# First group's x in four transfers, its statistics and normalization spread over other engines

## The chip, the core and the metric

The kernel runs on one NeuronCore of a Trainium2 chip. The metric is device time in microseconds (us) of one execution, the median of several runs. TensorE (PE in the profile, PEld for its weight loads), VectorE (DVE), ScalarE (ACT), GpSimd (POOL) and SyncE (SP, which here issues all transfers) each work through their own instructions in order, and wait for each other through semaphores.

## What is computed

x is 2048 tokens of 448 features. `xn` is its layer normalization over the features. The output is x + A(xn) + B(xn):

```python
# A: global filter in the frequency domain
X = rfft2(xn); y = irfft2(X * (w_r + 1j * w_i), s=(S, D))
# B: spatial-shift token mixing, then a channel MLP
h  = gelu(layernorm(xn) @ w1)                    # 448 -> 448
hs = concat(shift(h quarter 0, +1), shift(quarter 1, -1),
            shift(quarter 2, +2), shift(quarter 3, -2)) @ w2
x1 = xn + hs
out_B = x1 + gelu(layernorm(x1) @ w3) @ w4       # 448 -> 1792 -> 448
```

## The kernel before

Tokens are dealt to 16 blocks of 128 tokens, `xb(b)`, so that a shift by one token is a shift by one block. Two neighbouring blocks share a tile `xt`. Stage B goes by groups of four blocks: `GRP = [[14, 15, 0, 1], [2, 3, 4, 5], [6, 7, 8, 9], [10, 11, 12, 13]]`. Each fp32 operand of a matrix product is split into an fp16 high half and an fp16 low half, and a product is three matmuls (high by high, high by low, low by high).

Ahead of a split, a weight matrix is scaled by a power of two. `squares` sums its squares on ScalarE, one ACTIVATE and one accumulator read for each part. `powers` adds the sums (`tensor_reduce`, L243 on VectorE), spreads the total over the partitions with a matmul by ones (L245, here "the ones-matmul"), and makes the powers `s` and `r` in three small VectorE steps (L249 to L252). This happens four times, for w1, w2, w3 and w4 (s1 to s4).

The stretch that matters is the front:

- `load_x(0)` loads the four blocks of group 0 in two transfers (L192), then come w1 in four parts, the next groups' x, w2 and w3, all on SP's one queue.
- TensorE meanwhile runs `WARM` matmuls on zeros (L752).
- `norm1(g, apply)` normalizes a group: `stats` takes mean and variance of each block on VectorE (`bn_stats` L289, `bn_aggr` L290), five small steps (L306 to L311) make an approximate scale and a bias, and `apply` names the engine that applies them to each block (L319 on VectorE or POOL, L316 on ScalarE). The function `refine`, some ten small POOL steps (L328 to L337), makes the exact scale later.
- `T1(g)` transposes a group in four quarters of the features on TensorE (`pta`, L370). ScalarE copies each quarter as the high half of `xT` (L374), VectorE subtracts it for the low half (L375).
- `split_w` makes the halves of w1. For the first two quarters ScalarE scales and rounds (L264) and VectorE makes the low half (L265). For the last two POOL scales in place (L260), ScalarE rounds (L261) and POOL subtracts (L262). w2's four quarters all go by POOL.
- `w1_in` runs group 0's 44 matmuls (L410) into four banks. `w1_unit` applies gelu and splits h, and a transposing DMA (L434) turns h around. Then group 1 follows in the same way, and group 2.
- `w2_tile(b)` multiplies the four shifted quarters of h with w2 (L450), in the order 2, 0, 1, 3.

Much later come the MLP (L381, L716), then A, and the last MLP groups. L697 there splits the MLP's hidden tile.

The order on each engine is fixed when the program is built: a scheduler places the instructions by priority and by an estimate of its own, and `with behind(key):` keeps the instructions of a block behind a named earlier one on the same engine, for example

```python
    with behind("n", 0):
        s1, r1 = powers(m1, 4, "1", "mm")
```

keeps s1's steps behind group 0's applies on VectorE. So an edit at the front can move instructions further on in the order.

Of the kernel before, what the change touches and what calls it, by code (L numbers as in the profile page):

```python
# [23 lines left out]
CS = {b: 4 * g + i for b, (g, i) in WHERE.items()}  # L24
PASS = ((0, 0), (0, 1), (1, 0))
SHIFT = [1, -1, 2, -2]
WARM = 28
ZPRE = 2.0 ** -7
UPRE = 2.0 ** -3
VPRE = 2.0 ** -3  # L30
# [89 lines left out]
def body(tc, nc, x, wf, w1, w2, w3, w4, c_g, c_n, c_small, out):  # L120
    V, A, P, T, SY = nc.vector, nc.scalar, nc.gpsimd, nc.tensor, nc.sync
# [50 lines left out]
    xr = pw.tile([128, 904], F32, name="xr")  # L172
# [13 lines left out]
    ident = pc.tile([128, 128], F32, name="ident")  # L186
# [1 line left out]


    def load_x(g):  # L190
        for b0 in sorted(GRP[g])[::2]:
            SY.dma_start(xt[b0 // 2], xv[:, b0:b0 + 2])  # L192

    load_x(0)
    w1s = stage("w1s", F, 0).rearrange("p (t n) -> p t n", t=4)
# [38 lines left out]
    def squares(col, src, junk=None):  # L234

        n = src.shape[-1]
        junk = xr.bitcast(F16) if junk is None else junk
        A.activation(out=junk[:src.shape[0], :n], in_=src, func=AF.Square, scale=2.0 ** -20, accum_out=col)

    def powers(m, n, key, tag="acc"):  # L240

        t = pc.tile([128, 2], F32, name=f"pt{key}")
        V.tensor_reduce(out=t[:, 0:1], in_=m[:, :n], axis=AX.X, op=ALU.add)  # L243
        pm = bank(tag, f"pm{key}") if isinstance(tag, str) else tag
        i = T.matmul(pm[:, 0:1], ones, t[:, 0:1], start=True, stop=True)  # L245
# [5 lines left out]
        V.tensor_scalar(out=e[:, 1:2], in0=e[:, 0:1], scalar1=-1, scalar2=185 << 23, op0=ALU.mult, op1=ALU.add)  # L251
        V.tensor_scalar(out=e[:, 2:3], in0=e[:, 0:1], scalar1=1, scalar2=69 << 23, op0=ALU.mult, op1=ALU.add)  # L252
        return e.bitcast(F32)[:, 1:2], e.bitcast(F32)[:, 2:3]

    def absmax(out_, in_):
# [1 line left out]

    def split_w(hi, lo, src, s, low=None):
        if low is P:
            P.tensor_scalar(out=src, in0=src, scalar1=s, scalar2=0.0, op0=ALU.mult, op1=ALU.add)  # L260
            i = A.activation(out=hi, in_=src, func=AF.Copy)  # L261
            j = P.tensor_tensor(out=lo, in0=src, in1=hi, op=ALU.subtract)  # L262
            return i.ins, j.ins
        i = A.activation(out=hi, in_=src, func=AF.Copy, scale=s)  # L264
        j = V.scalar_tensor_tensor(out=lo, in0=src, scalar=s, in1=hi, op0=ALU.mult, op1=ALU.subtract)  # L265
        return i.ins, j.ins
# [17 lines left out]
    def stats(src, key, mv=None):  # L284
        if mv is None:
            mv = pc.tile([128, 4, 2], F32, tag="mv", bufs=3, name=f"mv{key}")
        for i, s in enumerate(src):
            st = pc.tile([128, 6], F32, tag="st", bufs=4, name=f"st{key}_{i}")
            V.bn_stats(out=st, in_=s)  # L289
            V.bn_aggr(out=mv[:, i, :], in_=st)  # L290
        return mv
# [5 lines left out]
    def norm1(g, apply):  # L297

        bs = GRP[g]
        n, b0 = len(bs), bs[0]  # L300
        mv = pc.tile([128, 4, 2], F32, name=f"mva{b0}")
        stats([xb(b) for b in bs], f"a{b0}", mv)
        a = pc.tile([128, 2 * n], F32, name=f"va{b0}")
        yi = pc.tile([128, 2 * n], I32, name=f"vy{b0}")
        y = yi.bitcast(F32)
# [5 lines left out]
        i = V.scalar_tensor_tensor(out=nm, in0=mv[:, :n, 0], scalar=-1.0, in1=y[:, n:], op0=ALU.mult, op1=ALU.mult)  # L311
        after["c", g] = (i.ins,)
        for k, b in enumerate(bs):
            y_, m_ = y[:, n + k:n + k + 1], nm[:, k:k + 1]
            if apply[k] is A:
                i = A.activation(out=xb(b), in_=xb(b), func=AF.Identity, scale=y_, bias=m_)  # L316
                after["na", g] = (i.ins,)
            else:
                i = apply[k].tensor_scalar(out=xb(b), in0=xb(b), scalar1=y_, scalar2=m_, op0=ALU.mult, op1=ALU.add)  # L319
# [4 lines left out]
        w, r = (pc.tile([128, 2 * n], F32, name=f"v{t}{b0}") for t in "wr")  # L324
# [38 lines left out]
    def transpose_split(srcs, dst, key, ts=range(4), at=0, tags=("tr",) * 4):  # L363
        c = slice(128 * at, 128 * at + 128 * len(srcs))
        for t in ts:
            pt = bank(tags[t], f"pt{key}{t}")
            w = 128 if t < 3 else 64
            with behind("T", key) if ("T", key) in after else contextlib.nullcontext():
                for i, s in enumerate(srcs):
                    m = T.transpose(pt[:w, 128 * i:128 * i + 128], s[:, 128 * t:128 * t + w], ident)  # L370
            after["T", key] = (m.ins,)
            pt = pt[:w, :128 * len(srcs)]
            lo = dst[:, 4 + t, c] if t < 3 else dst[64:128, 3, c]
            i = A.activation(out=dst[:w, t, c], in_=pt, func=AF.Copy)  # L374
            j = V.tensor_tensor(out=lo, in0=pt, in1=dst[:w, t, c], op=ALU.subtract)  # L375
            after[key, t] = after[key] = i.ins, j.ins

    def mlp_in(ps_out, wp, cols, xT, tok, ts=range(4)):
        for t in ts:
# [305 lines left out]
    acc, hs, rest = {}, {}, {}  # L685
# [64 lines left out]
    def warm_up(n):  # L750
        for i in range(n):
            T.matmul(wps, wsrc[:, 0:128], wsrc, start=True, stop=True)  # L752
# [6 lines left out]
    xTs = {}  # L759
    flat = lambda t: t.rearrange("p a n -> p (a n)")  # L760

    def T1(g, ts=range(4)):
        if g not in xTs:
            xTs[g] = p1.tile([128, 7, 512], F16, tag="xT", bufs=2, name=f"xT{g}")
        transpose_split([xb(b) for b in GRP[g]], xTs[g], f"a{g}", ts,
                        tags=("mm", "mm", "tr", "tr") if g == 2 else ("tr", "tr", "acc", "acc"))

    def w3_split(i):
        t, cl = i % 4, slice(896 * (i // 4), 896 * (i // 4) + 896)
        split_w(w3p[:, t, cl], w3p[:, 4 + t, cl], w3raw[:, t, cl], s3)  # L770

    def w4_split(f):
        split_w(w4p[0][:, 0, f:f + 2], w4p[0][:, 1, f:f + 2], w4raw[:, f:f + 2], s4)

    for t in range(3):
        squares(m1[:, t:t + 1], w1s[:, t])
    squares(m1[:64, 3:4], w1s[:64, 3])
    n1 = [norm1(0, [P, V, A, V])]
    with behind("n", 0):
        s1, r1 = powers(m1, 4, "1", "mm")  # L780
    h_alloc(0)
    first = [bank("mm" if k < 2 else "sp", f"pw1_0{k}") for k in range(4)]
    for t in range(4):
        with behind("p1"):
            T1(0, [t])
        with behind("a0", t):
            after["w1", t] = split_w(w1p[:, t], w1p[:, 4 + t], w1s[:, t], s1, P if t > 1 else V)
    h1 = pc.tile([128, 1], F32, name="h1")
    V.tensor_scalar(out=h1, in0=s1, scalar1=2.0 ** -5, scalar2=None, op0=ALU.mult)
    for t in range(4):  # L790
        w1_in(0, list(enumerate(first)), [t])
    n1[0][0]()
    with behind("w1", 1):
        n1.append(norm1(1, [P, V, A, V]))
    with behind("w1", 3):
# [2 lines left out]
    with behind("n", 1):  # L798
        s2, r2 = powers(m2, 1, "2", first[0][:, 448:512])
# [28 lines left out]
    with behind("a2"):  # L828
        n1 = [norm1(3, [P, P, P, P])]
# [97 lines left out]
    bs = [*range(12, 16), *range(8, 12), *range(8)]  # L927
    for n in range(17):
# [4 lines left out]
        if n:  # L933
            b = bs[n - 1]
# [30 lines left out]
```

## Time and profile before

| | |
|---|---|
| median of 3 runs | 420.48 us (420.2 to 420.87) |
| the profiled execution | 420.4 us |
| its span in the profile | 418.6 us |
| TensorE matmuls | 409.8 us, 98% of the span |
| VectorE | 291.6 us, 70% |
| ScalarE | 248.1 us, 59% |
| GpSimd | 118.6 us, 28% |
| granted TensorE clock | 1.0 |

Busy time is the union of an engine's instructions over the whole span. A matmul's record is longer than its place in the stream, since matmuls overlap, so the share of TensorE is not a share of its peak. Times in the views count from the start of the span. A row of the timeline gives start, duration, engine, line, operation, the tiles out<-in with their shapes, and how many instructions it merges. A row of the chain of waits gives start, duration, and what the end of the program waited for in that time. In a row by window stand the window, its length, the busy time of PE, PEld, DVE, ACT and POOL, the granted clock, the DMA engines' share and their GB/s. A row of transfers ends with their size and the median us from issue to landing.

### The profile page before, as it was taken

Reading aid. Unit: us, or ns where it says so; the run is one execution under the profiler, and the core shown is the slowest. Engines: PE = TensorE matmul, PEld = TensorE weight load, DVE = VectorE, ACT = ScalarE, POOL = GpSimd, SP = SyncE. Lnnn points to the kernel's source line nnn. Section 1 sums busy time; section 2 is a strip of 40 time slices with the busy share of each in tenths; the row PEclk is TensorE's granted clock in tenths of the full one; section 3 lists DMA queues with packets and bytes.
Section 4 is the critical chain, followed back from the end, with each engine's and each line's share of the span. In section 5 each row is a group of like instructions: output and inputs, shape, how many; then the busy total and the mean of one; then the engine's idle time right before and its main releaser. Section 6 shows DMA issues by size and latency. Waiting matters only on the chain.

```text
span 418.6 us, 8535 instructions
## 1 busy us (share of the span) xinstructions
PE 409.8 (98%) x3329; PEld 291.7 (70%) x3329; DVE 291.6 (70%) x615; ACT 248.1 (59%) x428; POOL 118.6 (28%) x204
## 2 busy tenths in 40 slices
PE   7999999999999999999999999999999999999996
PEld 3655555765668777776887887777776767577785
DVE  4888899798774766652689889865999529942112
ACT  4698869972758866632678888864534414422331
POOL 3876700101345746300031221211454203200000
DMA  8959982734761365315056555610001003331001
GB/s 271 362 174 175 275 174 95 132 78 90 191 156 50 89 234 165 93 41 140 14 142 173 149 144 142 177 39 2 2 2 68 22 2 132 134 133 40 5 0 45
DMA packets 51832, 47.61 MB, mean 114 GB/s; under 512 B 33936, under 2 KB 47056, under 8 KB 51792
## 3 DMA queue, kind: packets, MB, share of 16 engines
q1 hardware_dynamic: 51792, 47.07, 41.7%
q8 instruction: 26, 0.43, 0.4%
q14 instruction: 14, 0.11, 0.1%
HBM read 35.52 MB, written 3.67 MB: 94 GB/s over the span
## 4 chain that ended last, share of the span: by engine, by line
PE 72%; DVE 14%; DMA 6%; issue 5%; POOL 1%; ACT 1%; SPq 1%; POOLq 0%; DVEq 0%
PE pw L381 25%; PE acc L716 22%; PE pw L450 7%; PE pw L410 6%; PE ps L536 3%; PE pu L638 2%; PE pp L593 2%; PE px L610 2%; DMA xr<-x 1%; DVE w4p L265 1%; DMA out<-xr 1%; PE pta L370 1%; DMA x2mem<-y 1%; DVE xt L682 1%; DVE sta L289 1%
## 5 line engine op out<-in xcount | busy, mean ns | idle before, releaser
L381 PE MATMUL pw<-x2mem,w3p 128*128 128x256 f16 x1232 | 151.8, 273 | 0.0
L716 PE MATMUL acc<-w4p,hf 128*128 128x448 f16 (+1 forms) x714 | 140.0, 341 | 0.7 <-DVE hf L697 0.7
L381 PEld LDWEIGHTS <-w3p 128*128 128x128 f16 x1232 | 118.9, 98 | 23.1 <-issue 0.9
L716 PEld LDWEIGHTS <-hf 128*128 128x128 f16 x714 | 69.2, 98 | 49.2 <-DVE hf L697 1.6
L697 DVE SCALAR_TENSOR_TENSOR hf<-pw,h,hf 128x512 f16<-128x512 f32 x56 | 41.7, 747 | 55.5 <-ACT hf L696 55.3
L694 ACT ACTIVATE pw<-pw,pe 128x512 f32<-128x512 f32 x56 | 36.6, 655 | 70.5 <-PE pw L381 69.4
L450 PE MATMUL pw<-w2p,h 112*128 112x448 f16 x192 | 40.1, 352 | 0.8 <-DMA h<-hs 0.8
L696 ACT ACTIVATE hf<-pw,h 128x512 f16<-128x512 f32 x56 | 38.3, 686 | 1.4
L619 POOL TENSOR_TENSOR z<-te 128x450 f32<-128x450 f32 x16 | 16.3, 1016 | 74.0 <-DVE te L617 74.0
L410 PE MATMUL pw<-w1p,xT 128*128 128x448 f16 x176 | 35.3, 352 | 0.0
L450 PEld LDWEIGHTS <-h 112*128 112x128 f16 x192 | 18.7, 98 | 17.0 <-DMA h<-hs 1.0
L666 POOL TENSOR_TENSOR e<-e 128x226 f32<-128x226 f32 x16 | 13.9, 866 | 56.5 <-ACT e L663 45.3
L410 PEld LDWEIGHTS <-xT 128*128 128x128 f16 x176 | 16.9, 98 | 16.2 <-DVE xT L375 0.8
L600 ACT ACTIVATE pf<-pp 64x450 f16<-64x450 f32 x32 | 17.3, 540 | 16.7 <-DVE pf L601 8.2
L601 DVE TENSOR_TENSOR pf<-pp,pf 64x450 f16<-64x450 f32 x32 | 19.9, 622 | 5.3 <-ACT pf L600 5.0
L663 ACT ACTIVATE e<-pe 128x452 f32<-128x452 f32 x16 | 8.7, 547 | 15.6 <-DVE vh L674 12.3
L516 POOL TENSOR_TENSOR xr<-xf 128x452 f32<-128x452 f32 x8 | 9.7, 1208 | 28.3 <-issue 22.9
L615 ACT ACTIVATE te<-px 64x450 f32<-64x450 f32 x32 | 17.2, 538 | 0.5
L673 ACT ACTIVATE vh<-e 128x448 f16<-128x448 f32 x16 | 9.2, 574 | 14.0 <-DVE e L671 8.3
L519 POOL TENSOR_TENSOR f<-xr 128x452 f32<-128x452 f32 x16 | 16.1, 1028 | 0.6
L527 DVE TENSOR_TENSOR xh<-f,xh 128x452 f16<-128x452 f32 x16 | 11.8, 780 | 5.9 <-ACT xh L526 5.9
L681 PE MATMUL py<-vh,csm 128*128 128x448 f16 x48 | 13.5, 352 | 1.5 <-DVE vh L674 0.7
(163 smaller groups left out, 602.8 us busy)
## 6 DMA issues: line engine op xcount, KB each, us to landing
wc<-wf SPq DMA_DIRECT2D x32, 225.0 KB, 3.7
wl<-wf SPq DMA_DIRECT2D x8, 450.0 KB, 3.7
xt<-x SPq DMA_DIRECT2D x8, 448.0 KB, 8.2
xf<-x SPq DMA_DIRECT2D x8, 448.0 KB, 3.7
w3raw<-w SPq DMA_DIRECT2D x3, 896.0 KB, 12.8
xr<-x SPq DMA_DIRECT2D x12, 224.0 KB, 2.6
out<-xr SPq DMA_DIRECT2D x12, 224.0 KB, 2.0
gn<-c_g SPq DMA_DIRECT2D x16, 128.0 KB, 3.3
```

The costliest lines, as they stand in the source:

```text
L381: T.matmul(ps_out, wp[:, wi + t, cols], xT[:, xi + t, tok], start=t == 0 and wi + xi == 0, stop=t == 3 and wi == 4)
L410: T.matmul(pm[:, :D], xTs[g][:, xi + t, 128 * i:128 * i + 128], w1p[:, wi + t], start=t == 0 and p == 0, stop=t == 3 and p == 2)
L450: T.matmul(pm[:, :D], hT[g][:112, 4 * hi + k, o:o + 128], w2p[:, wi, k], start=n == 0, stop=n == 11)
L519: P.tensor_tensor(out=f[:, :, k:k + 2].rearrange("p b s d -> p s b d"), in0=u[:, :, 0], in1=u[:, :, 1], op=op)
L600: A.activation(out=hi, in_=src, func=AF.Copy)
L601: V.tensor_tensor(out=lo, in0=src, in1=hi, op=ALU.subtract)
L615: A.activation(out=e[64 * h:64 * h + 64], in_=px_[64 - 64 * h:128 - 64 * h, :2 * DF], func=AF.Copy)
L619: P.tensor_tensor(out=z, in0=t[:, 0], in1=t[:, 1], op=ALU.add)
L694: A.activation(out=pm, in_=pm, func=AF.Gelu_apprx_tanh, scale=r3)
L696: i = A.activation(out=h[:, 0], in_=pm, func=AF.Copy, scale=h3)
L697: j = V.scalar_tensor_tensor(out=h[:, 1], in0=pm, scalar=h3, in1=h[:, 0], op0=ALU.mult, op1=ALU.subtract)
L716: m = T.matmul(to, h[:, hi, o:o + 128], w4p[0][:, wi, f, r], start=f == 0 and n == 0, stop=f == 13 and n == 2)
```

## The change

Six edits, all at the front:

1. Group 0's x comes in four transfers, one for each block, in the order 14, 15, 0, 1.
2. Block 14's mean and variance are taken by two ScalarE ACTIVATEs with accumulators (Identity, then Square with the mean as its bias). POOL turns the mean's sign and scale. VectorE's `bn_stats` takes the other three blocks.
3. The apply of block 0 moves from ScalarE to VectorE, so that POOL applies block 14 and VectorE 15, 0 and 1.
4. `T1` is cut into its TensorE part (`turn_pe`) and its copies (`turn_copy`). For group 0 the first quarter's transposes stand ahead of the ones-matmul of s1, and the other three quarters behind it. The copies of a quarter stand behind the weight split of the quarter before it, and the first behind s1.
5. POOL's scalings of w1 stand ahead of group 0's `refine` (`after["ws"]`).
6. w2's quarters are split in the order 2, 0, 1, 3, and `WARM` is 26 instead of 28.

```diff
-WARM = 28
+WARM = 26
...
     def load_x(g):
-        for b0 in sorted(GRP[g])[::2]:
-            SY.dma_start(xt[b0 // 2], xv[:, b0:b0 + 2])
+        for b0 in GRP[g][::1 if g == 0 else 2]:
+            if g == 0:
+                SY.dma_start(xb(b0), xv[:, b0])
+            else:
+                SY.dma_start(xt[b0 // 2], xv[:, b0:b0 + 2])
...
-        stats([xb(b) for b in bs], f"a{b0}", mv)
+        if g == 0:
+            t = pc.tile([128, 1], F32, name="ms")
+            junk = xr[:, 0:D]
+            A.activation(out=junk, in_=xb(b0), func=AF.Identity, scale=-D ** -1.5, accum_out=t)
+            A.activation(out=junk, in_=xb(b0), func=AF.Square, scale=D ** -0.5, bias=t, accum_out=mv[:, 0, 1:2])
+            P.tensor_scalar(out=mv[:, 0, 0:1], in0=t, scalar1=-D ** 0.5, scalar2=None, op0=ALU.mult)
+        stats([xb(b) if g or b != b0 else None for b in bs], f"a{b0}", mv)
...
+    def turn_pe(g, t):
+        pt = bank((("mm", "mm", "tr", "tr") if g == 2 else ("tr", "tr", "acc", "acc"))[t], f"pta{g}{t}")
+        w = 128 if t < 3 else 64
+        with behind("T", g) if ("T", g) in after else contextlib.nullcontext():
+            for i, b in enumerate(GRP[g]):
+                m = T.transpose(pt[:w, 128 * i:128 * i + 128], xb(b)[:, 128 * t:128 * t + w], ident)
+        after["T", g] = (m.ins,)
+        return pt[:w]
+
+    def turn_copy(g, t, pt):
+        ...
+        i = A.activation(out=dst[:w, t], in_=pt, func=AF.Copy)
+        j = V.tensor_tensor(out=lo, in0=pt, in1=dst[:w, t], op=ALU.subtract)
+        after[f"a{g}", t] = after[f"a{g}"] = i.ins, j.ins
...
+    n1 = [norm1(0, [P, V, V, V])]
     for t in range(3):
         squares(m1[:, t:t + 1], w1s[:, t])
     squares(m1[:64, 3:4], w1s[:64, 3])
-    n1 = [norm1(0, [P, V, A, V])]
-    with behind("n", 0):
+    pts = [turn_pe(0, 0)]
+    with behind("n", 0), behind("T", 0):
         s1, r1 = powers(m1, 4, "1", "mm")
+    with behind("p1"):
+        pts += [turn_pe(0, t) for t in range(1, 4)]
     h_alloc(0)
     first = [bank("mm" if k < 2 else "sp", f"pw1_0{k}") for k in range(4)]
     for t in range(4):
-        with behind("p1"):
-            T1(0, [t])
+        with behind(*(("w1", t - 1) if t else ("s1",))):
+            turn_copy(0, t, pts[t])
         with behind("a0", t):
             after["w1", t] = split_w(w1p[:, t], w1p[:, 4 + t], w1s[:, t], s1, P if t > 1 else V)
...
-    n1[0][0]()
+    with behind("ws"):
+        n1[0][0]()
...
     with behind("na", 2):
-        for k in range(4):
+        for k in (2, 0, 1, 3):
             split_w(w2p[:, 0, k], w2p[:, 1, k], w2s[:112, k], s2[:112], P)
```

More of the change, by code (lines that the diff above doesn't have):

```diff
@@ L251, in powers @@
         V.tensor_scalar(out=e[:, 1:2], in0=e[:, 0:1], scalar1=-1, scalar2=185 << 23, op0=ALU.mult, op1=ALU.add)
-        V.tensor_scalar(out=e[:, 2:3], in0=e[:, 0:1], scalar1=1, scalar2=69 << 23, op0=ALU.mult, op1=ALU.add)
+        i = V.tensor_scalar(out=e[:, 2:3], in0=e[:, 0:1], scalar1=1, scalar2=69 << 23, op0=ALU.mult, op1=ALU.add)
+        after["s" + key] = (i.ins,)
         return e.bitcast(F32)[:, 1:2], e.bitcast(F32)[:, 2:3]
@@ L259, in split_w @@
         if low is P:
-            P.tensor_scalar(out=src, in0=src, scalar1=s, scalar2=0.0, op0=ALU.mult, op1=ALU.add)
+            i = P.tensor_scalar(out=src, in0=src, scalar1=s, scalar2=0.0, op0=ALU.mult, op1=ALU.add)
+            after["ws"] = (i.ins,)
             i = A.activation(out=hi, in_=src, func=AF.Copy)
@@ L287, in stats @@
         for i, s in enumerate(src):
+            if s is None:
+                continue
             st = pc.tile([128, 6], F32, tag="st", bufs=4, name=f"st{key}_{i}")
@@ L361, in behind, with T1 @@
             yield
-    def transpose_split(srcs, dst, key, ts=range(4), at=0, tags=("tr",) * 4):
-        c = slice(128 * at, 128 * at + 128 * len(srcs))
-        for t in ts:
[L366 to L376, printed above, removed]
+    def turn_pe(g, t):
[7 more added lines that the diff above has]
+    def turn_copy(g, t, pt):
+        w = 128 if t < 3 else 64
+        if g not in xTs:
+            xTs[g] = p1.tile([128, 7, 512], F16, tag="xT", bufs=2, name=f"xT{g}")
+        dst = xTs[g]
+        lo = dst[:, 4 + t] if t < 3 else dst[64:128, 3]
+        i = A.activation(out=dst[:w, t], in_=pt, func=AF.Copy)
+        j = V.tensor_tensor(out=lo, in0=pt, in1=dst[:w, t], op=ALU.subtract)
+        after[f"a{g}", t] = after[f"a{g}"] = i.ins, j.ins
+    def T1(g, ts=range(4)):
+        for t in ts:
+            turn_copy(g, t, turn_pe(g, t))
     def mlp_in(ps_out, wp, cols, xT, tok, ts=range(4)):
@@ L760, in body @@
     flat = lambda t: t.rearrange("p a n -> p (a n)")
[L762 to L766, printed above, removed]
     def w3_split(i):
```

## The prediction

> **What bounds the kernel now.** I read the page's chain first, then what TensorE waited for, then the chain in order of time for the first 70 us, then each engine's timeline there. From the page, and TensorE's waits over the whole span:
>
> ```profile
> span 418.6 us, 8535 instructions
> PE 72%; DVE 14%; DMA 6%; issue 5%; POOL 1%; ACT 1%; SPq 1%; POOLq 0%; DVEq 0%
> PE pm L245 <- DVE pt L243: 1.0, 1, 1.0
> PE pw L450 <- DMA h<-hs: 0.8, 1, 0.8
> ```
>
> TensorE is the chain. Everything the change edits lies ahead of the end of the last wait shown. After that TensorE starts matmuls back to back until far behind the reordered stretch, so what the front gains or loses reaches the end unshortened, unless a new gap opens. The chain of waits in order of time:
>
> ```profile
> 1.19 4.32 DMA xt<-x
> 5.53 2.21 DVE sta L289 x4
> 7.74 0.29 DVE mva L290 x4
> 8.94 0.93 DVE xt L319 x2
> 9.99 0.38 PE pm L245 x2
> 10.37 1.94 PE pta L370 x16
> 12.31 8.41 PE pw L410 x44
> 30.45 3.20 DMA h<-hs
> ```
>
> x lands at 5.51; four statistics, the applies, the ones-matmul for w1's power of two (s1), 16 transposes; from 12.31 to 20.7 the 44 matmuls of group 0 run at 0.19 us each. So the front is worth what those 44, and what follows them, start earlier.
>
> **x and the applies.** The rows of the pieces that move, from the timeline:
>
> ```profile
> 0.73 0.87 SPq L192 DMA_DIRECT2D xt<-x  x2
> 1.22 7.74 PE L752 MATMUL wps<-wsrc 128*128 128x512 f16 x28 [1.22 <-DVE wsrc L183]
> 9.05 0.19 ACT L238 ACTIVATION_READ_ACCUMULATOR xr<-w1s 64x1 f32 x1
> 9.12 1.17 POOL L319 TENSOR_SCALAR xt<-xt,vy,nma 128x448 f32<-128x448 f32 x1
> 43.50 2.82 POOL L319 TENSOR_SCALAR xt<-xt,vy,nma 128x448 f32<-128x448 f32 x4
> ```
>
> SP issues four transfers where it issued two: two more at 0.44 us push the w1 issues back 0.9 us. Call x the delay with which the data then land. Block 14, the first, goes to ScalarE: two ACTIVATEs (0.6, like L374's below) with an accumulator read of 0.19 each, about 1.5 us, hidden by the wait for w1, whose squares are ScalarE's next work and whose data come after x; POOL's one small instruction for the mean (0.2) is hidden by the statistics. That cover holds while block 14 lands before 4.8; each us later than that would hold up the applies by one. VectorE does the other three as they land, so behind the last landing stands one statistic (0.55 a piece) where there were four: three less is 1.6, and three of the four aggregates 0.2. The applies start at 8.94-1.8=7.15+x. VectorE has three, one each 0.43 after the other, done at 8.5. POOL's apply of block 14 starts 0.19 later and takes 0.70 alone (2.82/4) and 1.17 beside two VectorE applies: 0.23 for each, 1.4 beside three, so it ends at 8.75+x. That cover is thin but costs nothing: the transposes that wait for it then run 8.8 to 9.3, while s1 is still to come. The 26 warm-up matmuls end two of 28 earlier (0.28 each on the mean), at 8.4: still ahead of those transposes, so they cost and bring nothing.
>
> **s1 and the weights.** The rows that carry the sum:
>
> ```profile
> 9.79 0.15 DVE L243 TENSOR_REDUCE pt<-m 128x1 f32<-128x4 f32 x1
> 10.79 0.15 DVE L251 TENSOR_SCALAR pe<-pe 128x1 int32<-128x1 int32 x1
> 11.04 0.60 ACT L374 ACTIVATE xT<-pta 128x512 f16<-128x512 f32 x1 [1.15 <-PE pta L370]
> 11.54 0.66 ACT L264 ACTIVATE w1p<-w1s,pe 128x448 f16<-128x448 f32 x1
> 12.28 0.68 DVE L265 SCALAR_TENSOR_TENSOR w1p<-w1s,pe,w1p 128x448 f16<-128x448 f32 x1
> 14.06 2.20 DVE L289 BATCH_NORM_STATS2 sta<-xt 128x6 f32<-128x448 f32 x4
> 14.51 1.25 POOL L260 TENSOR_SCALAR w1s<-w1s,pe 128x448 f32<-128x448 f32 x2
> 19.11 1.17 POOL L319 TENSOR_SCALAR xt<-xt,vy,nma 128x448 f32<-128x448 f32 x1
> 20.57 1.47 PE L370 MATMUL pta<-ident,xt 128*128 128x128 f32 x12
> 26.84 0.56 DVE L803 TENSOR_TENSOR s<-h,pe 128x1 f32<-128x1 f32 x1
> 27.33 0.15 DVE L804 SCALAR_TENSOR_TENSOR s<-pe,pe 128x1 f32<-128x1 f32 x1
> ```
>
> The last square of w1 is read at 9.24+x. L243 stood behind the applies until 9.79; now it starts at 9.27+x, and its chain of 1.15 us gives s1 at 10.42+x instead of 10.94. ScalarE has copied xT's first quarter before that (9.6 to 10.2), so its first w1 half starts with s1 and ends at 11.1+x instead of 12.2. TensorE does four transposes, the ones-matmul at 9.47+x (0.38), then twelve transposes at 0.12 (16 took 1.94): it reaches group 0's matmuls at 11.3+x instead of 12.3. So TensorE gains 1.0-x here.
>
> VectorE gains less. After s1 it does xT's low quarter (0.69, to 11.15+x), then w1's low half. But POOL's two scalings of w1 (L260, 0.63 each) move from 14.51 to right behind s1: 10.47 to 11.73+x. L803, 128x1, takes 0.56 us while POOL's scaling of w2 runs, its like L804 0.15: a VectorE instruction with two inputs in SBUF sits out the POOL instruction under way. w1's low half has two such inputs, so I let it wait until 11.73+x. At a pitch of 0.6 it, xT's second and w1's second low half follow, and group 1's statistics start at 13.5+x instead of 14.06: 0.57-x earlier. (The Trainium skill says this in "SBUF — State Buffer", section "Who interferes with whom": VectorE with two SBUF inputs and a GpSimd instruction that reads SBUF exclude each other, and whichever starts first holds the port to its end. It speaks against this change, and L803 agrees with it. Without the rule the sum would be 1.0-x.) From there VectorE's steps are the old ones, so POOL's apply of block 2, which ended at 20.28, ends at 19.7+x; group 1's transposes need it and start at 19.76+x. TensorE had finished group 0 at 19.57+x. Gain: 20.57-19.76-x = 0.8-x.
>
> **x.** Bounds: SP's lag of 0.9 if the issue decides, and about 0 if the transfers are simply full. What the queue moved, by window (the last column is GB/s):
>
> ```profile
> 3.00:3.50 0.50, 0.50 (x3) 0.21 (x2) 0.00 (x0) 0.00 (x0) 0.00 (x0) 1.00 1.14 394
> 5.00:5.50 0.50, 0.50 (x4) 0.20 (x3) 0.00 (x0) 0.00 (x0) 0.00 (x0) 1.00 1.03 301
> xr<-x SPq DMA_DIRECT2D x12, 224.0 KB, 2.6
> ```
>
> The first is x in rows of 3584 bytes, the second w1 in rows of 1792, as x's will be. All of x (0.92 MB) at 301 instead of 394 GB/s would be 0.7 us more. Against it, a lone 224 KB block of x elsewhere lands 2.6 us after its issue, so the first would be there at 3.3, and three more at 301 GB/s (0.76 each) make 5.6 for the last, 0.1 later than now. I take x=0.2, near this row, and the range 0 to 0.7.
>
> **w2's quarters, and where the stretch ends.**
>
> ```profile
> 31.20 1.04 POOL L262 TENSOR_TENSOR w2p<-w2s,w2p 112x448 f16<-112x448 f32 x1
> 32.42 3.01 POOL L262 TENSOR_TENSOR w2p<-w2s,w2p 112x448 f16<-112x448 f32 x3
> 33.16 2.67 SPq L434 DMA_TRANSPOSE h<-x2mem  x2
> 33.69 0.36 PE L450 MATMUL pw<-w2p,h 112*128 112x448 f16 x1 [0.77 <-DMA h<-hs]
> ```
>
> Each tile of w2 begins with quarter 2, whose low half was POOL's third; now it is ready at 32.2 instead of 34.4, and two more matmuls (0.38) fit into TensorE's wait. That buys nothing: the next blocks of h come from SP's transposes, one every 1.37 us, and before too TensorE met the fourth of them as it landed (issued 33.16). What counts is when the second was issued (30.45), and that hangs on VectorE, whose work the chain follows from group 1's transposes on nearly without a pause. The 0.8-x arrives there whole. Sum: 0.8-0.2=0.6. The profiled execution took 420.4 (span 418.6 and 1.8 around it); the median shown is 420.48. Forecast: 420.4-0.6=**419.8**.
>
> **Rivals.** (1) *The front gains fully*: VectorE's low half slips in ahead of POOL's scaling and x is 0. TensorE then sets the start: gain 1.0. In the mid part the only gap of note may also close:
>
> ```profile
> 121.58 1.69 PE L716 MATMUL acc<-w4p,hf 128*128 128x448 f16 x8 [0.38 <-DVE hf L697]
> ```
>
> 0.5 us with its start. 418.9 to 419.4. For it: only 0.1 us lies between the two starts in my sum. Against: POOL needs nothing but s1.
>
> (2) *It does nothing*: the data lag by the whole 0.9 us of issue. Gain 0.8-0.9: 420.5. For it: the transfers' ramp is slow, and if it counts rows and not bytes, half-size rows carry half as much. Against: the w1 data waited behind x, not for their issue. ("DMA: Bandwidth & Descriptors", section "Bandwidth", in the Trainium skill, asks for transfers of 1 MiB and more; by it four blocks lose against two. Here four in flight share one queue, and 2.6 us for a lone block is mostly latency.)
>
> (3) *Slower: a wait moves into the full stretch.* The built order changes from 31 to 125 us. The ones-matmul of w4's power of two (86.75 before) now stands behind 43 fewer matmuls of w3 (256 columns) and 11 fewer of w2 (448): at the 0.191 us that group 0's 448 columns take, and 0.109 for 256, 6.8 us earlier, at 80.0. It needs ScalarE's seventh square of w4 and VectorE's L243:
>
> ```profile
> 80.15 1.22 ACT L481 ACTIVATE y<-y,vs 128x448 f16<-128x448 f32 x2
> 82.11 0.19 ACT L238 ACTIVATION_READ_ACCUMULATOR xr<-x2mem 128x1 f32 x1
> 84.41 0.16 DVE L243 TENSOR_REDUCE pt<-m 128x1 f32<-128x7 f32 x1
> 86.75 0.28 PE L245 MATMUL pm<-pt,ones 128*128 128x1 f32 x2
> ```
>
> With these times TensorE would stand for 84.6-80.0=4.6 us: 424.4. But ScalarE's new order puts four normalizations (L481, 0.61 each) behind that square, which then is read at 82.3-2.4=79.9, and VectorE's order brings L243 forward behind it: just in time. Each us later than 80.0 costs one us; from 0.6 on the front's gain is gone. VectorE's 2.1 us between the read and L243 show how late it may come: a loss of up to 2.1-0.6=1.5, so 420.5 to 421.9.
>
> **The numbers.** Chances: forecast 0.45, (1) 0.30, (2) 0.08, (3) 0.17. 0.2% of 420.48 is 0.84 us, about what a measurement of this kernel can tell from no change. The forecast's own range (x 0 to 0.7) is 419.6 to 420.3, a gain of 0.1 to 0.8, inside the 0.84 but at its better end close to it; of its 0.45 I give 0.07 to the far side. Of (3)'s 0.17, 0.05 is a small loss within the 0.84. Faster 0.30+0.07=0.37, same 0.38+0.08+0.05=0.51, slower 0.12. The range 418.8 to 421.2 takes in (1), (2) and half of (3).
>
> **What would show it.** Right: group 0's first w1 matmul near 11.4, its transposes from 9.0, s1 near 10.6, group 1's transposes near 20.0, w1's first low half on VectorE over 1 us long, and behind 37 us no new gap on TensorE. Wrong: w1's squares read at or after 9.9 (my x too small); that low half no longer than L265's 0.68 and group 1's transposes at 19.6 (rival 1); a wait of TensorE on L246, the new line of L243, near 80 us (rival 3); a first w1 matmul slower than 0.19 us, which would be a clock not granted.

## The result and the profile after

The change made the kernel slower: 422.04 us median (421.55 to 422.89) against 420.63 (420.2 to 421.07) for the kernel before in the same runs, ratio 1.0041 with a 95% interval of 1.0032 to 1.0049. The forecast was 419.8. The profiled execution took 421.97 us. From the page and from TensorE's waits of the kernel after:

```profile
span 420.2 us, 8541 instructions
PE 410.7 (98%) x3327; PEld 291.7 (69%) x3327; DVE 291.4 (69%) x614; ACT 249.3 (59%) x431; POOL 117.0 (28%) x205
```

```profile
PE pta L381 <- POOL xt L332: 1.6, 2, 0.9
...
PE pw L471 <- DMA h<-hs: 0.8, 1, 0.8
```

By its share of the span no engine is busier than before; TensorE has 0.9 us more and ScalarE 1.2. TensorE now waits twice for an apply on POOL (L332), 1.6 us in all, where it waited 1.0 for L243. TensorE's timeline, before (first fence) and after (second), shows where the time went; rows give start, duration and the idle time ahead in brackets:

```profile
12.24 8.48 PE L410 MATMUL pw<-w1p,xT 128*128 128x448 f16 x44
```

```profile
10.48 0.66 PE L381 MATMUL pta<-ident,xt 128*128 128x128 f32 x4 [0.71 <-POOL xt L332]
11.28 0.38 PE L248 MATMUL pm<-pt,ones 128*128 128x1 f32 x2
11.52 1.51 PE L381 MATMUL pta<-ident,xt 128*128 128x128 f32 x12
12.99 8.48 PE L431 MATMUL pw<-w1p,xT 128*128 128x448 f16 x44
22.35 1.53 PE L381 MATMUL pta<-ident,xt 128*128 128x128 f32 x12 [0.88 <-POOL xt L332]
```

Group 0's w1 matmuls start at 12.99 instead of 12.24, 0.75 late. Group 1's transposes start at 22.35 instead of 20.57, another 1.0 late. Counted by the matmuls done, TensorE is 1.55 us behind at 40 us, about 1.6 at 80 us, and 1.45 at the last matmul, which ends at 416.84 instead of 415.38. So both losses are at the front and stay.

**First loss: the data.** ScalarE's timeline of the kernel after; its squares of w1 (L241) stood at 6.28, 6.98, 7.87 and 8.57 before:

```profile
3.40 0.58 ACT L312 ACTIVATE xr<-xt 128x448 f32<-128x448 f32 x1 [1.17 <-DMA xt<-x]
...
8.78 0.58 ACT L241 ACTIVATE xr<-w1s 128x448 f16<-128x448 f32 x1 [0.22 <-DMA w1s<-w]
...
9.66 0.58 ACT L241 ACTIVATE xr<-w1s 128x448 f16<-128x448 f32 x1 [0.22 <-DMA w1s<-w]
...
10.36 0.58 ACT L241 ACTIVATE xr<-w1s 64x448 f16<-64x448 f32 x1
```

Block 14 is there at 3.4 and its statistics are done at 4.9, but w1's fourth square starts 1.79 late. In the trace x is complete at 7.11 (5.51 before) and w1's fourth part at 10.20 (8.25). The row of the four transfers, and what the queue moved in three windows, after (first three rows) and before (the last column is GB/s, the one ahead of it the DMA engines' busy share):

```profile
xt<-x SPq DMA_DIRECT2D x4, 224.0 KB, 3.8
```

```profile
3.50:4.50 1.00, 1.00 (x4) 0.30 (x2) 0.54 (x1) 0.97 (x3) 0.24 (x1) 1.00 0.83 172
4.50:5.50 1.00, 1.00 (x4) 0.34 (x3) 0.09 (x1) 0.36 (x2) 0.00 (x0) 1.00 0.96 296
5.50:6.50 1.00, 1.00 (x4) 0.41 (x3) 0.00 (x0) 0.00 (x0) 0.00 (x0) 1.00 0.93 287
```

```profile
3.50:4.50 1.00, 1.00 (x5) 0.32 (x3) 0.00 (x0) 0.00 (x0) 0.00 (x0) 1.00 0.92 373
4.50:5.50 1.00, 1.00 (x6) 0.46 (x5) 0.00 (x0) 0.00 (x0) 0.00 (x0) 1.00 1.00 332
5.50:6.50 1.00, 1.00 (x7) 0.47 (x5) 0.97 (x2) 0.23 (x1) 0.00 (x0) 1.00 0.97 348
```

After the first two blocks the flow falls to 172 GB/s for a microsecond: in the trace 8 to 14 packets are under way at a time from 3.3 to 4.4 us, where it is mostly 16 before and after, although the third block has been issued since 2.1. The first two blocks land 2.65 and 2.75 us after the start of their issue, blocks 0 and 1 4.85 and 4.99 after it; the median is 3.8, not 2.6.

**Second loss: POOL's queue.** Its timeline after:

```profile
12.40 0.64 POOL L264 TENSOR_SCALAR w1s<-w1s,pe 128x448 f32<-128x448 f32 x1 [1.97 <-DVE pe L255]
13.96 0.64 POOL L264 TENSOR_SCALAR w1s<-w1s,pe 128x448 f32<-128x448 f32 x1 [0.92 <-ACT xT L391]
14.56 0.57 POOL L341 TENSOR_TENSOR vq<-vy 128x8 f32<-128x8 f32 x1
...
16.60 1.03 POOL L267 TENSOR_TENSOR w1p<-w1s,w1p 128x448 f16<-128x448 f32 x1
...
17.76 1.03 POOL L267 TENSOR_TENSOR w1p<-w1s,w1p 128x448 f16<-128x448 f32 x1
...
21.09 0.20 POOL L358 TENSOR_TENSOR cs<-cs,vw 128x4 f32<-128x4 f32 x1
...
21.58 0.71 POOL L332 TENSOR_SCALAR xt<-xt,vy,nma 128x448 f32<-128x448 f32 x1
```

VectorE's timeline after:

```profile
11.07 0.16 DVE L246 TENSOR_REDUCE pt<-m 128x1 f32<-128x4 f32 x1 [0.39 <-ACT xr L241]
...
12.97 0.69 DVE L270 SCALAR_TENSOR_TENSOR w1p<-w1s,pe,w1p 128x448 f16<-128x448 f32 x1
...
14.17 0.89 DVE L270 SCALAR_TENSOR_TENSOR w1p<-w1s,pe,w1p 128x448 f16<-128x448 f32 x1
...
19.83 0.93 DVE L332 TENSOR_SCALAR xt<-xt,vy,nma 128x448 f32<-128x448 f32 x2
```

VectorE is ready to apply group 1's normalization at 19.83, but POOL begins its block at 21.58: the steps of group 0's `refine` and `scales` (14.56 to 21.3), which before stood in POOL's gaps ahead of the scaling, now stand between the scaling and the apply. The scaling is late in turn: its second half waits until 13.8 for w1's last part (13.81 in the trace, 11.51 before), which is the 11th transfer now. In both kernels SP issues the ninth and every later transfer only once the one eight places before has landed (the 11th at 6.52, the third landed at 6.50). This is an order of the program, not of the queue: in the trace the transfers take turns at eight semaphores, and each waits for the earlier transfer that has its own.

### The profile page after: what moved, and what is told of

Read it like the earlier page. It is cut to its first block, busy times and chain, and to the rows that moved or that the text cites. A ratio compares the mean times of both kernels' runs of the same rounds, so it can differ in the third digit from the quotient of the medians.

```text
span 420.2 us, 8541 instructions
## 1 busy us (share of the span) xinstructions
PE 410.7 (98%) x3327; PEld 291.7 (69%) x3327; DVE 291.4 (69%) x614; ACT 249.3 (59%) x431; POOL 117.0 (28%) x205
## 4 chain that ended last, share of the span: by engine, by line
PE 55%; DVE 8%; issue 3%; DMA 2%; ACT 1%; POOL 1%; DVEq 0%
PE pw L402 23%; PE acc L737 22%; PE ps L557 3%; PE pu L659 2%; PE pp L614 2%; PE px L631 2%; DMA xr<-x 1%; DMA out<-xr 1%; DVE xt L703 1%; DVE xr L514 1%; DVE e L689 1%; DVE vh L695 1%; DVE e L691 1%; DVE e L690 1%; DVE x2mem L514 1%
## 5 line engine op out<-in xcount | busy, mean ns | idle before, releaser
L621 ACT ACTIVATE pf<-pp 64x450 f16<-64x450 f32 x32 | 17.3, 541 | 16.6 <-DVE pf L622 8.1
L548 DVE TENSOR_TENSOR xh<-f,xh 128x452 f16<-128x452 f32 x16 | 12.7, 835 | 6.8 <-ACT xh L547 6.8
```

## Experiments

In each, the time is set against the kernel before on the same chip in the same runs. POOL's `behind("ws")` is the line that puts `refine` behind the scaling.

**Data and POOL's order, one at a time.** Two transfers in the order of use:

```diff
-        for b0 in GRP[g][::1 if g == 0 else 2]:
...
+        for b0 in GRP[g][::2]:
+            SY.dma_start(xt[b0 // 2], xv[:, b0:b0 + 2])
```

> The changed kernel with group 0's x loaded by two transfers of two blocks each (14 and 15, then 0 and 1) where it had four. Theory D (the data): the four half-size transfers are what delays x (7.11 instead of 5.51) and w1 (10.20 instead of 8.25). Then here x's last block lands near 5.5, w1's fourth part near 8.3, s1 is there near 10.4 and group 0's first w1 matmul starts near 11.3 (13.0 in the changed kernel). POOL keeps its new order, 7.0 us of it between the end of its second scaling of w1 and its apply for group 1, so that this apply ends near 20.5 and group 1's transposes start there: 420.5 us. Theory P (POOL's order alone): the transfers cost nothing that counts, since POOL is what group 1 waits for; group 1's transposes stay near 22.2 and the time near 422.0.

420.44 us, ratio 0.9991 (0.9981 to 1.0001). POOL's and TensorE's timeline:

```profile
11.21 1.76 POOL L261 TENSOR_SCALAR w1s<-w1s,pe 128x448 f32<-128x448 f32 x2 [1.57 <-ACT xT L388]
...
19.73 0.70 POOL L329 TENSOR_SCALAR xt<-xt,vy,nma 128x448 f32<-128x448 f32 x1
```

```profile
11.80 8.48 PE L428 MATMUL pw<-w1p,xT 128*128 128x448 f16 x44
20.49 1.53 PE L378 MATMUL pta<-ident,xt 128*128 128x128 f32 x12 [0.21 <-POOL xt L329]
```

With two transfers x is complete at 5.79 and w1's fourth part lands at 8.50. Group 1's transposes and the time are where theory D had them; the first w1 matmul is 0.5 later than its 11.3. The two scalings take 1.76 instead of 1.25: the second started at 11.90, under VectorE's low half of w1 (11.78 to 12.47), and took 1.07. POOL still ends last at group 1.

`refine` free, transfers as in the change:

```diff
-    with behind("ws"):
-        n1[0][0]()
+    n1[0][0]()
```

> The changed kernel, but group 0's second Newton steps on POOL need not stand behind the scaling of w1: they go ahead of it, as before the change. Theory P (POOL's order costs a part): POOL's apply for group 1 starts with VectorE's at 19.8 instead of 21.58, TensorE reaches group 1's transposes at 21.3 without a wait: 0.7 to 0.9 less, 421.2 us. Theory D alone (everything lost is the data's delay): group 1's transposes start at 22.2 all the same and the time stays at 422.0.

421.51 us, ratio 1.0020 (1.0004 to 1.0036):

```profile
13.02 8.48 PE L431 MATMUL pw<-w1p,xT 128*128 128x448 f16 x44
21.34 1.36 PE L381 MATMUL pta<-ident,xt 128*128 128x128 f32 x11
```

```profile
19.82 1.18 POOL L332 TENSOR_SCALAR xt<-xt,vy,nma 128x448 f32<-128x448 f32 x1
```

Theory P: the first loss stays (13.02), the second is gone, POOL's apply starts with VectorE's. The median is above the 421.2 of theory P; four of the twelve executions, 422.25 to 423.3, have a mean granted clock of 0.996 (see below).

Both edits together:

> Both of the other two edits: two transfers for group 0's x and POOL's Newton steps ahead of its scaling of w1. If data and POOL's order are the two costs, what was meant to be gained is left: first w1 matmul near 11.3, group 1's transposes near 19.6, 1.0 us ahead of the kernel before: 419.7 us. If something else in the change costs (a block's statistics on ScalarE, the applies without ScalarE, the copies' order), it stays at 420.6 or above.

419.96 us, ratio 0.9975 (0.9965 to 0.9986), and in a second set 419.94 against 420.9, 0.998 (0.9971 to 0.9988). That is faster than both kernels. TensorE in the second set:

```profile
11.63 8.48 PE L428 MATMUL pw<-w1p,xT 128*128 128x448 f16 x44
19.96 1.47 PE L378 MATMUL pta<-ident,xt 128*128 128x128 f32 x12
```

The front gains 0.61. So there was a gain to be had at the front, under two costs.

The other way round, the kernel before with four transfers only:

> The kernel before, with only group 0's x loaded by four transfers of one block, in the order 14, 15, 0, 1. Theory D: x's last block lands near 7.1 and w1's fourth part near 10.2, s1 is there near 12.2 instead of 10.94, the first w1 matmul starts near 13.2, group 1's transposes near 21.6: 421.7 us. Theory P: group 1's transposes hang on POOL and on group 1's statistics, which are as before: 420.6 to 420.9.

422.5 us (421.96 to 425.39), ratio 1.0051 (1.0030 to 1.0072), worse than theory D had it. x was complete at 7.48 and w1's fourth part at 10.28, near what was expected. What was not: the w1 matmuls started at 15.14 in the profile, not 13.2, at half the granted clock (the sixth value behind the window's length):

```profile
14.00:16.00 2.00, 2.00 (x10) 1.35 (x9) 2.00 (x4) 2.00 (x6) 2.00 (x4) 0.50 1.06 282
```

Five of eleven executions have a mean granted clock of 0.992 to 0.996 and took 423.8 to 425.4 us; the six with 0.999 or 1.0 took 422.0 to 422.5, 0.3 to 0.8 above the 421.7 of theory D. And POOL's order alone:

```diff
+            after["ws"] = (i.ins,)
...
+    with behind("ws"):
+        n1[0][0]()
```

> The kernel before, with only POOL's order changed: group 0's Newton steps stand behind the scaling of w1. Theory D and P together: the data are on time, the second scaling ends near 12.3 to 13.0, the 7.0 us of POOL's work behind it push its apply for group 1 from 19.11 to 19.3 to 19.9, ending 20.0 to 20.6; group 1's transposes start 20.4 to 20.7 (20.57 before): 420.6 to 420.9 us. Rival (POOL's order costs its full 1.1 us wherever the data are): near 421.8.

421.24 us, ratio 1.0009 (1.0000 to 1.0019). POOL's apply starts at 20.10 instead of 19.11, TensorE's transposes at 20.86 instead of 20.57. Of these 0.29 us, 0.15 stand already at group 0's w1 matmuls (12.39 instead of 12.24). So with the data on time POOL's order costs between 0.1 and 0.3 of the 1.0 us in the profile; the rest needs the late scaling.

**Why the data are late.** Two tiny transfers more, nothing split:

```diff
+    dum = pc.tile([128, 2], F32, name="dum")
+    for i in range(2):
+        SY.dma_start(dum[:, i:i + 1], xv[:, i, 0:1])
```

> The kernel before with two more transfers of 512 bytes each, of x into a tile that nobody reads, issued by SP between group 0's x and w1. Theory issue: the two extra issues of 0.47 us each and the two places they take are what delays w1; w1's fourth part lands 0.9 us later than 8.25, the slack of 0.55 before s1 is used up: 421.0 us. Theory size: the delay comes from moving x in half-size transfers; with these two w1's fourth part lands by 8.5 and the time is 420.6.

421.09 us, ratio 1.0014 (1.0001 to 1.0028). x is not late (5.42), w1's fourth part lands at 8.84, its square starts 0.47 later than before (8.57):

```profile
9.04 0.58 ACT L241 ACTIVATE xr<-w1s 64x448 f16<-64x448 f32 x1
```

Issue and places explain 0.6 of w1's 1.95. Of x the run says nothing, since the two tiny transfers stand behind it. The last part of w1, 11th here too, lands at 13.69 (13.81 in the change, 11.51 before), so its delay does not need a split x. In the profile the lag of w1 stays inside the slack at s1, and group 0's w1 matmuls start at 12.16, as before. The median's 0.2 us are not explained by it.

Four transfers with long rows:

```diff
+            for h in range(2 if g == 0 else 1):
+                p = slice(64 * h, 64 * h + 64) if g == 0 else slice(0, 128)
+                SY.dma_start(xt[b0 // 2][p], xv[p, b0:b0 + 2])
```

> The changed kernel with group 0's x in four transfers again, but each carries 64 partitions of two blocks, in rows of 3584 bytes, where the changed kernel has 128 partitions of one block in rows of 1792. Theory rows: short rows are what is slow; then x is complete near 5.6 and w1's fourth part near 8.8: 421.0 us. Theory number: four transfers of 224 KB are slower than two of 448 KB whatever their rows, x is complete near 7.1 and w1's fourth part near 10.2: 422.0 us.

422.44 us, ratio 1.0038 (1.0024 to 1.0051). x is complete at 7.49, w1's fourth part lands at 9.93:

```profile
10.29 0.58 ACT L240 ACTIVATE xr<-w1s 64x448 f16<-64x448 f32 x1
```

The landing times are near those of theory number, but the run does not prove it. The transfers were issued by 3.2 us, at 0.6 us each instead of 0.43, so that a part of the delay is issue. And the flow falls in another way than in the change, with the DMA engines fully busy:

```profile
3.50:4.50 1.00, 1.00 (x4) 0.29 (x2) 0.00 (x0) 0.00 (x0) 0.00 (x0) 1.00 1.00 244
4.50:5.50 1.00, 1.00 (x6) 0.49 (x5) 0.35 (x1) 0.36 (x1) 0.00 (x0) 1.00 1.01 222
```

Long rows on half of the partitions may be slow for a reason of their own, so short rows are not ruled out as a cause in the change. Three of the four executions also lost the clock (0.996; 422.25 to 422.97); the one with 1.0 took 421.75. The Trainium skill, "DMA: Bandwidth & Descriptors", section "Rules for kernel authors", advises against two transfers to two halves of the partitions, since both run over the same 16 engines; this run agrees (x complete at 7.49, against 5.79 with two transfers on all partitions). That four transfers in place of two delay x and w1 is shown, by taking them out of the changed kernel and by putting them into the kernel before; why the third of them lands late stays open.

The last part of w1 ahead of group 1's x:

```diff
-    load_x(1)
     SY.dma_start(w1s[64:128, 3], w1[384:448])
+    load_x(1)
```

> The changed kernel with the repeated half of w1's fourth part (rows 384 to 448, the 11th transfer) issued ahead of group 1's x. SP issued each transfer from the ninth on 0.02 us after the transfer eight places before it had landed; as the ninth this one is not held up and lands near 11 instead of 13.81. Theory slots: POOL's second scaling of w1 then starts right behind the first, at 13.04 instead of 13.96, everything behind it on POOL comes 0.9 earlier and TensorE no longer waits for it at group 1's transposes: 421.1 us. Theory port: VectorE's low half of w1 (12.97 to 13.66) holds POOL's second scaling until 13.7 all the same, so that only 0.3 us is won: 421.7 us.

422.77 us, ratio 1.0047 (1.0034 to 1.0060). The part lands at 10.60, POOL's two scalings run from 12.42 to 14.12 and its apply starts at 20.97, 0.61 earlier: more than theory port's 0.3, less than theory slots' 0.9. The second scaling took 1.08 under VectorE's low half. But the time rose. TensorE and its granted clock:

```profile
10.44 0.66 PE L381 MATMUL pta<-ident,xt 128*128 128x128 f32 x4 [1.49 <-POOL xt L332]
...
13.71 9.35 PE L431 MATMUL pw<-w1p,xT 128*128 128x448 f16 x44
```

```profile
12.40:15.00 2.60, 2.60 (x12) 1.71 (x11) 2.58 (x6) 2.60 (x6) 2.45 (x4) 0.50 1.10 226
```

The warm-up had ended at 8.95, TensorE stood, and from 12.0 to 15.4 its clock was halved: transposes at 0.21 instead of 0.109, w1 matmuls at 0.37 instead of 0.19.

**The clock.** Four more warm-up matmuls on the changed kernel, the same on the last kernel, and then the changed kernel without and with them on one chip:

```diff
-WARM = 26
+WARM = 30
```

> The changed kernel with 30 warm-up matmuls where it has 26. With the last part of w1 loaded earlier, TensorE stood 1.5 us between its last warm-up matmul and the first transposes, and its granted clock was 0.50 from 12 to 15.2 us. Theory clock: the same happens in some executions of the changed kernel, whose runs went from 421.55 to 422.89; four more matmuls keep TensorE busy until the transposes, and the median comes down to the fast end, 421.6 us. Theory data alone: TensorE waits there for data whatever it does before, and the median stays at 422.0.

> The kernel with the last part of w1 issued ahead of group 1's x, and 30 warm-up matmuls. There POOL's apply for group 1 ended at 21.68 instead of 22.29, and that gain was covered by the slow clock. Theory clock: with TensorE kept busy the 0.6 us come through, group 1's transposes start near 21.7: 421.1 us, 1.6 less than with 26. Theory data alone: no change from 422.8.

> The changed kernel itself, on one chip with the three others of this set. In the set before, x and w1 landed 0.4 to 0.6 us earlier than in the changed kernel's own profile, and the kernel before was 0.4 us faster, so that ratios of different sets can't be set against each other to some tenths of a microsecond. Theory clock: runs spread over more than 1 us, those with a mean granted clock of 0.995 to 0.996 at the slow end. About 1.4 us above the kernel before.

> The changed kernel with 30 warm-up matmuls, beside the changed kernel on the same chip. Theory clock: no run with a mean clock under 0.998, and a median 0.4 to 1.0 us below the changed kernel's. Theory data alone: the same median as the changed kernel's.

In the first of these, with data 0.6 us earlier than in the change's own profile, 30 matmuls gave 420.79 against 420.31, ratio 1.0015 (1.0006 to 1.0023). The second kernel gave 421.24, 1.0020 (1.0011 to 1.0029), where 26 had 1.0047; group 1's transposes start at 21.99 instead of 22.89. On one chip: the changed kernel 422.65, 1.0041 (1.0028 to 1.0054), with 30 matmuls 422.3, 1.0027 (1.0018 to 1.0037). Of six executions of the changed kernel four have a mean clock of 0.995 or 0.996 (422.58 to 423.68), two have 1.0 (421.58 and 422.1). With 30 none of nine is under 0.999 (421.25 to 422.66). The changed kernel's profile of this set, timeline and window:

```profile
11.42 0.66 PE L381 MATMUL pta<-ident,xt 128*128 128x128 f32 x4 [1.88 <-POOL xt L332]
...
14.01 4.30 PE L431 MATMUL pw<-w1p,xT 128*128 128x448 f16 x15
```

```profile
13.80:16.00 2.20, 2.20 (x8) 1.03 (x7) 2.20 (x4) 2.20 (x5) 0.99 (x2) 0.50 1.09 237
```

And with 30:

```profile
10.66 0.66 PE L381 MATMUL pta<-ident,xt 128*128 128x128 f32 x4 [0.33 <-POOL xt L332]
```

```profile
12.00:14.00 2.00, 2.00 (x16) 1.44 (x15) 1.95 (x7) 1.64 (x4) 0.63 (x1) 1.00 1.03 213
```

So a late x costs twice: it lets TensorE stand behind its warm-up, and in some executions the clock is then halved for 3.4 us. The two matmuls that the change cut are not a condition of it, since the kernel before with four transfers, which has all 28, lost the clock too. On one chip the cover was worth 0.35 us of median, below the expected 0.4 to 1.0, and the two intervals overlap; that no execution has the low clock is the clearer evidence.

**What the rest is worth.** Block 14's statistics back on VectorE, from the kernel with both edits, in two sets:

```diff
-        if g == 0:
...
-        stats([xb(b) if g or b != b0 else None for b in bs], f"a{b0}", mv)
+        stats([xb(b) for b in bs], f"a{b0}", mv)
```

> The kernel with two transfers for group 0's x (14 and 15 first) and POOL's Newton steps ahead of its scaling, 419.96 us, with block 14's statistics back on VectorE. VectorE has two statistics of 0.55 each to do between the landings of the two transfers, 1.1 us apart, and did only one there. Theory order: the statistics on ScalarE bring nothing, what helps is that VectorE no longer waits for all four blocks: 419.9 us. Theory ScalarE: taking a statistic off VectorE is worth its 0.8 us: 420.5 or more.

> Two transfers for group 0's x and POOL's Newton steps ahead of its scaling of w1, on the same chip as the next: 0.6 us below the kernel before.

> The last one with block 14's statistics on VectorE, on the same chip. Theory order (the statistics on ScalarE bring nothing): the same time within 0.2 us. Theory ScalarE: 0.4 us or more slower, as the ratios of the two sets (0.9975 and 0.9992) would have it.

First set 419.99 against 420.31, 0.9992 (0.9983 to 1.0001); second, on one chip, 420.1 against 419.94 with the statistics on ScalarE, ratios 0.9983 (0.9974 to 0.9991) and 0.9980. The statistics on ScalarE bring nothing that can be measured; in the second set's profile the w1 matmuls even start at 11.38 without them and at 11.63 with them. In the first set's profile VectorE does two blocks between the two landings, and two behind, without a gap:

```profile
4.32 1.15 DVE L293 BATCH_NORM_STATS2 sta<-xt 128x6 f32<-128x448 f32 x2 [3.00 <-DMA xt<-x]
...
5.61 1.12 DVE L293 BATCH_NORM_STATS2 sta<-xt 128x6 f32<-128x448 f32 x2
```

The kernel before with the order of the loads and `[P, V, V, V]` alone:

```diff
-        for b0 in sorted(GRP[g])[::2]:
+        for b0 in GRP[g][::2]:
...
-    n1 = [norm1(0, [P, V, A, V])]
+    n1 = [norm1(0, [P, V, V, V])]
```

> The kernel before, with two edits: group 0's two transfers in the order in which their blocks are used (14 and 15 first), and the third apply on VectorE instead of ScalarE; transposes and copies of the change are left out. s1 then hangs on w1's squares, read at 9.24, and is there near 10.45 instead of 10.94; the sixteen transposes still stand together behind the ones-matmul, and the first w1 matmul starts near 11.9 instead of 12.31: 420.3 us. If the order of transposes and copies is what earns the gain of the kernel with 419.96, this one stays at 420.6.

420.23 us, ratio 0.9998 (0.9989 to 1.0007). The w1 matmuls start at 11.95, as expected, 0.29 earlier, but the median shows nothing; 0.3 us lie inside its interval. How much of the gain belongs to the order of transposes and copies is not settled by it. Then the kernel with both edits, with w2's quarters as before, and with the two loads in the old order:

```diff
-        for k in (2, 0, 1, 3):
+        for k in range(4):
```

> The kernel with two transfers for group 0's x and POOL's Newton steps ahead of its scaling (ratio 0.998), with w2's quarters on ScalarE and POOL in the order 0, 1, 2, 3 again. Theory waits: TensorE waits behind group 2's transposes for h, whichever quarter is ready, so the order of the quarters is worth nothing: ratio 0.998. Theory order: the first tile of w2 waits for quarter 2's low half, POOL's third, and 0.4 to 0.9 us is lost: ratio 0.999 to 1.000.

```diff
-        for b0 in GRP[g][::2]:
+        for b0 in sorted(GRP[g])[::2]:
```

> The same kernel with group 0's two transfers in the order they had before the change, 0 and 1 first, 14 and 15 after. Theory order of loads: block 14 lands at 5.5, ScalarE's two passes over it end near 7.1 and hold up the squares of w1 by 0.8 us, VectorE has one statistic behind the second landing; s1 comes 0.4 to 0.8 later: 420.5 us, ratio 0.9995 or more. Theory order of work: the gain comes from transposes and copies placed ahead, whatever comes first; ratio 0.998.

w2 as before: 420.22 against 420.5, 0.9992 (0.9983 to 1.0001). Loads as before: 420.14, 0.9994 (0.9985 to 1.0003), w1 matmuls at 12.10 instead of 11.63. Both give back about 0.5 us of the median; each interval meets that of 0.998, so the sizes are loose, and the profiles do not bear out the whole of it: with the loads as before the front is 0.47 later, yet that profile's last matmul ends at 414.70, the other's at 415.17. One profile is one execution, and executions of one kernel differ by as much. For w2's order TensorE's wait behind group 2's transposes is longer by 0.19 with the old order (first row) than with the new (second):

```profile
33.55 0.36 PE L468 MATMUL pw<-w2p,h 112*128 112x448 f16 x1 [1.21 <-DMA h<-hs]
```

```profile
33.71 1.31 PE L468 MATMUL pw<-w2p,h 112*128 112x448 f16 x6 [1.02 <-DMA h<-hs]
```

## Why the prediction was wrong

**x was mis-sized.** It was taken as 0.2, at most 0.7; x was complete 1.60 late and w1 1.95. The step that failed is the bound from a lone block: 2.6 us from issue to landing held for the first two of the four (2.65 and 2.75), not for the third and fourth (4.85 and 4.99). I had treated the queue as a pipe with a rate, and the rival "it does nothing" as bounded by the 0.9 us of issue. In the trace the last block is issued 0.93 us later than the second pair was before (2.12 and 1.19) and takes 0.67 longer to land (4.99 and 4.32). The prediction had a figure near each, 0.9 for the issue and 0.7 for the shorter rows, but took them as alternatives; that they add up to x's delay does not show that these are its causes. The sign that the prediction named for it came: w1's squares were read at 11.04, not before 9.9. The group 0 step then follows, so its mechanism was right: with w1's last square 1.80 late, s1 came at 12.3 where the sum has 10.42+x, and the w1 matmuls at 12.99 where it has 11.3+x.

**POOL was left out of group 1.** "From there VectorE's steps are the old ones, so POOL's apply of block 2 ... ends at 19.7+x" looked at VectorE alone. Moving the scalings ahead of `refine` moves `refine` behind them, into the stretch ahead of POOL's next apply: it ended at 22.29. This was to be read from the order of POOL's instructions. It costs 1.0 in the change; freeing `refine` took it away. A slower kernel was expected from rival 3 alone, and neither of these two losses is in it.

**The warm-up was said to "cost and bring nothing".** That sum put its end at 8.4 with a mean of 0.28 per matmul, one moment for all executions. In the profiles the step from 0.43 to 0.216 us per matmul came between 4.2 and 7.2 us, so a warm-up of 26 ended between 8.5 and 9.9, and with late data the wait behind it reached 1.9 us in the changed kernel, long enough to lose the clock.

**The port.** I let VectorE's first low half wait for POOL's second scaling. It took 0.69 (at 12.97): it came ahead of that scaling, as rival 1 had it. In the change the second scaling still waited for w1's last part; in the kernels where it did not, it came just behind the low half and waited itself (1.07 and 1.08 instead of 0.64). The second low half, 0.89, began behind a scaling (14.17 and 13.96) and shows VectorE held by 0.2. The rule of "SBUF — State Buffer", section "Who interferes with whom", in the Trainium skill agrees with both: whichever starts first keeps the port. So the mechanism is there, but the forecast had the wrong one first, although its two starts at group 1 lay only 0.19 apart (19.57 and 19.76, not the 0.1 of rival 1's text).

**w2's order** ("That buys nothing"): 0.2 us at the wait in the profiles, more by the medians, not settled.

**Right:** block 14's statistics and the early transposes lie beside other work; s1's chain of small steps takes 1.23 us (11.07 to 12.30; 1.15 forecast); nothing was lost in the reordered stretch: TensorE does not wait for L246 near 80 us, and rival 3 is out. That the gain at the front is 0.61 once both costs are out, where the sum had 0.8-0.2, is luck: in that kernel x comes in two transfers, `refine` stands ahead of the scalings, and TensorE goes from group 0 to group 1 without a wait, while the sum had POOL's apply set that start. What the stretch behind makes of the 0.61 is not clear: in that profile TensorE waits 0.38 at 122.89 for a VectorE step of the first fold, 0.74 with the small gaps around it, where the kernel before stood 0.54, and of 0.64 us at 40 us 0.2 are left at the end, while the medians are 0.7 to 1.0 apart.

## What to carry to other kernels

Before a load is split so that work can begin on its first piece, ask when the last piece lands and what is queued behind it: here the first block came 1.0 us earlier than a pair, x as a whole 1.6 later and the weights 1.95 later, while two transfers, the pair that is used first ahead, had x complete by 5.8 us and w1 near 8.5. An instruction moved ahead in an engine's queue moves others behind it; follow those to the next thing that is waited for. And where a warm-up is trimmed, set its end against the latest time at which the first real matmul may come.

## What was unexpected of the hardware

- The granted clock fell to 0.50 for 3.41 us in the four profiles in which TensorE had stood longest between warm-up and transposes: 1.5 us (12.0 to 15.4), 1.9 (13.2 to 16.6), 2.2 (the kernel before with four transfers) and 2.9 (the half partitions). After 1.0 us (the kernel before) and 0.7 us (the changed kernel's own profile) it did not. The Trainium skill, "TensorE: Matmul & The Clock Gate", Part 1, gives a free-running window of about 3.4 us and an idle window as the condition; the length agrees, but an idle time of half of it was enough here.
- In all four the fall came 6.83 us, twice 3.41, after the trace's first record of the full clock, wherever the wait lay. In the second of these two windows TensorE had been idle for 1.6 to 2.7 us; in every other profile, for 1.07 at most. If such windows count, the start of the full clock, which differs by 3 us between profiles, decides how a wait is shared out among them, and with it which executions lose the clock. No run tests this.
- The trace has no record of the clock before the warm-up matmuls step from 0.43 to 0.216 us each (the first begins at 6.86 in the changed kernel's profile, the step is at 6.74). The views print 1.00 there, so a granted clock of 1.00 in the first microseconds is no sign of full speed.
- With four transfers, w1's fourth part landed at 9.56, 10.20 and 10.92 in three profiles from three sets (x at 6.54, 7.11 and 8.03), and the kernel before took 420.31 and 420.9 us in the first and the last set: as much as most of these edits are worth.
